# A weight's sign and rounded tail in one word, its sum on VectorE or GpSimd, and a new order of issue, in an attention and softplus-FFN kernel

## The chip, the cores and the metric

The kernel runs on one core of a Trainium2 chip. The metric is the device time of one execution in microseconds (us), the median of several runs. The core has five engines with a queue each: TensorE (PE, matrix products), VectorE (DVE), ScalarE (ACT), GpSimd (POOL) and SyncE (SP, which here issues every DMA). They run side by side and wait for one another through semaphores. Each queue is strictly in order: an instruction that waits holds up everything behind it.

## The reference

```python
# q, k, v: (4, 8, 768, 64) float32; block = 32, window = 16
k_sum = k.reshape(B, H, nb, block, D).max(axis=3)          # 24 block keys: the maximum
v_sum = v.reshape(B, H, nb, block, D).mean(axis=3)         # 24 block values: the mean
scores_l = where(|i - j| < window, scale * q @ k.T, -1e9)
scores_s = scale * q @ k_sum.T + log(block)
a = softmax(concatenate([scores_l, scores_s]))             # over 768 + 24 keys
x = (a @ concatenate([v, v_sum])).reshape(3072, 512)       # the heads side by side
h = x @ w_in                                               # 512 x 2048
g = maximum(h, 0) + log1p(exp(-abs(h)))                    # softplus
out = g @ w_out                                            # 2048 x 512
```

`w_in` and `w_out` arrive as 64-bit floats, two 32-bit words an element; all else is float32.

## The kernel before

**Chunks and phases.** The 3072 tokens are 12 chunks of 256. A group of one or two chunks is fed forward together: groups `[0,1] [2] [3,4] [5,6] [7,8] [9,10] [11]`, numbered x = 0 to 6. The hidden dimension is cut into 16 slices of 128, f = 0 to 15. For each group and slice TensorE makes `ph = w_in[f]·x` (L845, `product`), ScalarE the softplus twice from PSUM (`gh` rounded, L868, and the exact one, L872), VectorE the difference `gl` (L876, `rest`), and TensorE adds `g·w_out[f]` into `po` (L883, `project`). Operands are split into a high and a low part (`xh`, `xl`; `gh`, `gl`; the weight `w` in two halves), and each product takes three matmuls. Below, "f0.10" is slice 10 of group 0. Groups 0 and 1 go through slices 0 to 10 first and come back for 11 to 15, since the weights are still being converted.

**Attention.** A unit is one chunk with four of the eight heads: scores (`sc`, L612), mask and row minimum on VectorE (L625), exp on ScalarE (L633), the inverse of the sum (L641), normalizing on VectorE or GpSimd (L646), a transpose, values (`xo`, L706), then `xh` and `xl` (L722, L729). The four units of group 0 (a0.0.0, a0.0.2, a0.1.0, a0.1.2) transpose on TensorE (`pt`, L659) and copy to `pT` (L663); later units go through DRAM (`squares`). The first product of the kernel needs a0.0.0 and half of w0. Until then TensorE's gaps are filled with `warm` products (L965).

**Weights.** For each f the function `weights` loads w_in[f] and w_out[f] as raw words (L755, L758; for f = 0 and 1 separately, 512 columns each; from f = 2 together, 1024 columns) and makes a float32 by integer steps: magnitude (mask of the upper word, L771 on VectorE or L774 on ScalarE), `clamp` (L778), `shift` left by 3 (L782), `sign` (L786, the sign and top exponent bit of the upper word, or-ed in), `tail` (L792 on ScalarE or L795 on VectorE: the lower word over 2^29, rounded to 0..8, in place), `add_tail` (L800, GpSimd: an exact integer add), `high` (L804, a rounding copy into `w`) and `low` (L811, the remainder, on VectorE or GpSimd). The raw words of w6 to w15 lie where the first group's attention keeps its inputs, so these loads come after it. Temporaries (`t` of the weights, `kf`, `st`, `ob`) share a ring of two buffers, tag "t"; a load into the ring waits in SP's queue until the buffer two before it is free.

**Order.** Every step is a `Task` with one or several ways (engine and function). `SEQUENCE`, a table of 1623 numbers, is the order in which the tasks are issued; a letter after a number takes the second or third way ("a", "b"). DMAs go round eight semaphores, so each waits until the one eight before it has landed.

Of the kernel before, what the change touches and what calls it, by code (L numbers as in the profile page):

```python
# [12 lines left out]
U32 = mybir.dt.uint32  # L13
I32 = mybir.dt.int32
# [133 lines left out]
43 44 0 3 4 5 6 2 7 154 155 156 157 145 158 159 160 8 45 146a 46 9 10 11 12 13 14 15 82 64 68 16 17 150 147 148  # L148
161 149 162 18 19 163 151 20 144 47 49 21 22 23 78 51 164a 168 24 25 92 93 48 152 94 26 27 28 29 1 30 165 166
167 50 169 170 172 177 95 52 31 153 96 173a 104 105 106 174 171 53 175 176 55 72 54 56 75 116 97 98 99 117 118  # L150
59 57 100 61 58 60 62 89 86 128 63 85b 32 71b 81b 604 178 107 108a 181 179a 180 119 33 109 34 35 111 36 37 38
605 129 120 67 182 183 184 185 186 39 40 65 69 70 66 101 130 131 187 188 417 41 608 609 83 80 84 79 191 192 140
141 142 424 425 77b 102 103 110 112 76 87 74b 189 426 73 438 42 201 113 114a 115 190 616 143 202 321 335 336 121
122 132 123 124 193 194 195 427 196 322 323 125 126a 127 324 325 428 133 445 134a 617 90 197 198 622 624 135 349
88b 211 337 338 339 91b 136 418 419 212 207 221 326 222 423 203 204 205 206 328 350 137 138 351 352 327 340 139
429 421 342 446 208 199 329 330 343 430 341 353 354 200a 331 332 333 344 345 612 251 431 434 420 346 209 210 355
623 433 432 213 214 215 216 447 448 217a 356 357 449a 231 232 358 334 361 362 363 613 364 347 422 621 348 359
360 367 365 223 224 630a 218 366 225 227 219 220 625 368 371 226 228 369 435 370 241 450 633 372 233a 234 235
237 229 242 252 436 451 236 439 441 230 444 261 262 452 437 648 243a 238 244 245 246 373 379 374 375 377 247 647
380 381 376 378 248 382 271 272 440 291 651 239 240 249 250 253 254 255 256 257 383 384 263a 385 634 391 386 387  # L160
388 264 265 258 656 649 392 389 390 395 266 259 260 650 393 394 277 267 442 453 443 454 455 456 457 268 659 458
269a 270 397 396 403 311 606 607a 635 398 399 636 401 400 610 674 611a 678 404 405 614 281 618 626 637 615 406
402 638 459 660 465 292 629 619 460 466 467 461 462 410 407 411a 468 409 408 412a 293 661 662 294 620 675 282
413 312 471 463 464 469 470 472 473 295 477 297 478 479 475 474 483 484 485 476 481 296 663a 298 299 480 486 301
673 273 274 639 489 490 491 275 276 492 664 482 495 496 497 498 278 487 488 493 494 501 507 279 300 502 503 414
415a 280a 508 504 681 283 284 287 509 628 640 510 513 499 514 317 515 285 286 500 505 302 519 516 520 631 643
528 521 288 506 289 511 512 517 696 416 697 700a 641 695 682 518 703 824 823 825 665 303 304 305 529 627 290 826
# [17 lines left out]
1070 1278a 1271 822 976 974 977 1076 975 1071 1089 1088 1090 978 979 980 982 988 1079 1111 1133 1134 1135 983
989 984 1272 990 985 1078 1260 991 981 986 1091 1092 1258 1259 1269 1273 1112 1281 1136a 1137 1093 1282 1283
1284 994 987 1000 992 995 993 1001 996 1285a 997 998 1295 1296 1099 1100 1298 999 1113 1101 1115 1138 1286 1002
1003 1261 1004 1005 1006 1007 1008 1009 1012 1013 1102 1116 1014 1304a 1299 1105 1104 1114 1117 1125 1139 1140
1287 1130 1141 1118 1119 1015 1010 1011 1128 1018 1127 1016 1131 1126 1019 1017 1024 1297 1307 1020 1025 1021
# [17 lines left out]
1465 1526 1468 1464 1469 1535 1536 1527 1466a 1528 1533 1532 1537 1538 1541 1542 1543 1544 1547 1548 1549 1534  # L207
# [8 lines left out]
def kernel(  # L216
# [521 lines left out]
    def weights(f):  # L738
        order.group = f"w{f}"

        for i0, i1 in [(0, 1), (1, 2)] if f < 2 else [(0, 2)]:
# [19 lines left out]
            def word(up, dtype, raw=raw):  # L761
                return raw()[:, :, up].bitcast(dtype)
# [22 lines left out]
            def sign(t=t, word=word):  # L785
                nc.vector.scalar_tensor_tensor(  # L786
                    t(), word(1, U32), 0xC0000000, t(), ALU.bitwise_and, ALU.bitwise_or,
                )
# [255 lines left out]
```

## Time and profile before

| | |
|---|---|
| median of 3 runs | 620.74 us (620.58 to 621.48) |
| the profiled execution | 621.56 us, of which the span from first to last instruction is 619.8 us |
| TensorE busy | 608.5 us (98%), granted clock 0.994 in the mean |
| VectorE, ScalarE, GpSimd busy | 273.8 us (44%), 306.8 us (50%), 95.3 us (15%) |
| `add_tail` on GpSimd (L800) | 18 instructions, 41.8 us |
| `sign` on VectorE (L786) | 18 instructions, 19.8 us |
| bytes moved by DMA | 85.33 MB |

Busy time is time with an instruction running. A matmul counts as busy while it waits in the array, so the share of TensorE says little; whether it has gaps is read from the start times of its products. The page's lines by stage show that VectorE and ScalarE are full in the first 100 us and half idle later.

### The profile page before, as it was taken

Reading aid. Unit: us, or ns where it says so; the run is one execution under the profiler, and the core shown is the slowest. Engines: PE = TensorE matmul, PEld = TensorE weight load, DVE = VectorE, ACT = ScalarE, POOL = GpSimd, SP = SyncE. Lnnn points to the kernel's source line nnn. Section 1 sums busy time; section 2 is a strip of 40 time slices with the busy share of each in tenths; the row PEclk is TensorE's granted clock in tenths of the full one; section 3 lists DMA queues with packets and bytes.
Section 4 is the critical chain, followed back from the end, with each engine's and each line's share of the span. In section 5 each row is a group of like instructions: output and inputs, shape, how many; then the busy total and the mean of one; then the engine's idle time right before and its main releaser. Section 6 shows DMA issues by size and latency. Waiting matters only on the chain.

```text
span 619.8 us, 11379 instructions
## 1 busy us (share of the span) xinstructions
PE 608.5 (98%) x4384; PEld 506.8 (82%) x4384; DVE 273.8 (44%) x752; ACT 306.8 (50%) x758; POOL 95.3 (15%) x86
## 2 busy tenths in 40 slices
PE   7989999999999999999999999999999999999997
PEld 6678888988888888888888888888888888888996
DVE  5999997777454335544235221321333202211111
ACT  4998786748463255656637234631354314312322
POOL 4454533543100010112102004000000000000000
PEclk8899999999999999999999999999999999999999
DMA  9888985843557356464436145340533200210100
GB/s 304 252 272 275 316 266 132 268 139 113 160 186 255 96 160 191 118 210 145 144 117 207 38 142 123 88 128 1 143 98 106 73 1 2 76 59 0 69 1 34
DMA packets 83765, 85.33 MB, mean 138 GB/s; under 512 B 24608, under 2 KB 69504, under 8 KB 83712
## 3 DMA queue, kind: packets, MB, share of 16 engines
q1 hardware_dynamic: 83712, 84.62, 44.6%
q8 instruction: 34, 0.56, 0.4%
q14 instruction: 19, 0.16, 0.1%
HBM read 64.23 MB, written 18.35 MB: 133 GB/s over the span
## 4 chain that ended last, share of the span: by engine, by line
PE 78%; issue 1%; POOL 1%; ACT 0%; DVE 0%; POOLq 0%
PE po L883 37%; PE ph L845 36%; PE xo L706 3%; PE sc L612 2%; POOL t L800 1%; POOL w L811 0%; ACT ob L926 0%; DVE gl L876 0%; POOLq L800 0%; POOLq L811 0%
## 5 line engine op out<-in xcount | busy, mean ns | idle before, releaser
L845 PE MATMUL ph<-xh,w 128*128 128x512 f32 (+1 forms) x920 | 259.5, 355 | 1.0 <-DVE gl L876 0.9
L883 PE MATMUL po<-w,gh 128*128 128x512 f32 x768 | 201.4, 392 | 0.0
L845 PEld LDWEIGHTS ph<-xh,w 128*128 128x128 f32 x920 | 164.9, 189 | 27.6 <-DVE gl L876 1.7
L868 ACT ACTIVATE gh<-ph 128x512 fp32r<-128x512 f32 (+1 forms) x115 | 60.7, 528 | 230.3 <-PE ph L845 210.8
L876 DVE TENSOR_TENSOR gl<-ph,gh 128x512 fp32r<-128x512 f32 (+1 forms) x115 | 68.2, 599 | 233.7 <-ACT ph L872 233.1
L883 PEld LDWEIGHTS po<-w,gh 128*128 128x128 f32 x768 | 142.5, 188 | 29.9 <-issue 0.3
L845 PE MATMUL ph<-xl,w 128*128 128x512 f32 (+1 forms) x460 | 163.0, 354 | 0.4 <-DVE xl L729 0.4
L883 PE MATMUL po<-w,gl 128*128 128x512 f32 x384 | 113.5, 392 | 0.0
L845 PEld LDWEIGHTS ph<-xl,w 128*128 128x128 f32 x460 | 86.8, 189 | 13.4 <-DVE xl L729 0.6
L883 PEld LDWEIGHTS po<-w,gl 128*128 128x128 f32 x384 | 70.8, 188 | 14.4 <-DVE t L782 0.2
L633 ACT ACTIVATE sp<-sp,nm 128x120 f32<-128x120 f32 x192 | 73.1, 382 | 1.2 <-DVE nm L625 0.9
L872 ACT ACTIVATE ph<-ph 128x512 f32<-128x512 f32 (+1 forms) x115 | 59.0, 520 | 0.0
L800 POOL TENSOR_TENSOR t<-t,raw 128x1024 int32<-128x1024 int32 (+1 forms) x18 | 41.8, 2323 | 65.7 <-DVE t L786 16.1
L625 DVE CUSTOM_DVE_ANT_0 sp<-sc,added 128x120 f32<-128x120 f32 x192 | 40.7, 277 | 10.9 <-PE sc L612 10.6
L646 POOL TENSOR_TENSOR sp<-sp,ss 128x960 f32<-128x960 f32 x12 | 22.6, 1881 | 99.6 <-DVE ss L641 99.6
L633 ACT ACTIVATION_READ_ACCUMULATOR sp<-sp,nm 128x1 f32 x192 | 35.9, 187 | 0.0
L729 DVE TENSOR_TENSOR xl<-xo,xh 128x512 fp32r<-128x512 f32 x24 | 16.4, 682 | 37.5 <-ACT xh L722 37.3
L363 POOL TENSOR_TENSOR st<-st 96x512 f32<-96x512 f32 (+1 forms) x14 | 14.1, 1010 | 120.5 <-DMA st<-v_hp_dram 54.2
L868 ACT ACT_TABLE_LOAD x21 | 26.9, 1283 | 9.8 <-PE ph L845 9.5
L722 ACT CAST xh<-xo 128x512 fp32r<-128x512 f32 x22 | 12.9, 587 | 32.2 <-PE xo L706 32.2
L633 ACT ACT_TABLE_LOAD x18 | 23.1, 1283 | 7.4 <-DVE nm L625 7.2
L675 DVE STREAM_TRANSPOSE tb<-sp 128x1024 f32<-128x1024 f32 x20 | 24.8, 1238 | 1.5 <-POOL sp L646 1.1
(70 smaller groups left out, 391.8 us busy)
## 6 DMA issues: line engine op xcount, KB each, us to landing
squares<-tb SPq DMA_DIRECT2D x20, 512.0 KB
pT<-squares SPq DMA_DIRECT2D x80, 128.0 KB
raw<-w_out_dram SPq DMA_DIRECT2D x16, 512.0 KB
raw<-w_in_dram SPq DMA_DIRECT2D x16, 512.0 KB
kf<-kT_dram SPq DMA_DIRECT2D x16, 384.0 KB
out_dram<-ob SPq DMA_DIRECT2D x11, 512.0 KB
q<-qT_dram SPq DMA_DIRECT2D x20, 256.0 KB
st<-v_hp_dram SPq DMA_DIRECT2D x12, 384.0 KB
```

The lines of the kernel that those rows point to most:

```text
L625: nc.vector.tensor_tensor_reduce(out=sp()[:, n], in0=unit(n), in1=added()[:, kinds.index((lows[w], lows[w + 1]))], scale=-SCALE, scalar=FL ...
L633: nc.scalar.activation(sp()[:, n], sp()[:, n], AF.Exp, bias=nm()[:, n:n + 1], scale=-1.0, accum_out=ss()[:, n:n + 1],)
L646: engine.tensor_tensor(sp(), sp(), s, op=ALU.mult)
L675: nc.vector.transpose(out=tb().rearrange("p k (u q) -> p u k q", q=SQ), in_=tiles.sp().rearrange("p u (k q) -> p u k q", q=SQ),)
L706: nc.tensor.matmul(xo()[h * D:(h + 1) * D, g * CH + w * QW:g * CH + (w + 1) * QW], lhsT=tiles.v(g)[:, w, h * D:(h + 1) * D], rhs=queries(g ...
L729: nc.vector.tensor_sub(out=of_x(xl), in0=of_bank(), in1=of_x(xh).bitcast(F32))
L800: nc.gpsimd.tensor_tensor(a, a, word(0, I32), op=ALU.add)
L845: nc.tensor.matmul(ph()[:, :n], lhsT=w1()[:, i1, low, cc * P:(cc + 1) * P], rhs=a()[:, cc, cols], start=cc == 0 and i == 0, stop=cc == NCC ...
L868: nc.scalar.activation(gh()[:, cols], ph()[:, :n], AF.Softplus)
L872: nc.scalar.activation(ph()[:, :n], ph()[:, :n], AF.Softplus)
L876: nc.vector.tensor_sub(out=gl()[:, cols], in0=ph()[:, :n], in1=gh()[:, cols].bitcast(F32))
L883: nc.tensor.matmul(po[t](), lhsT=a()[:, t * P:(t + 1) * P], rhs=w2()[:, i2, low], start=f == f0 and i == 0, stop=f == f1 - 1 and i == 2,)
```

## The change

The upper raw word is reduced in place to its top two bits (`sign`, now a one-source instruction that writes `raw`). The rounded tail, 0..8, is written as 16 bits into the low half of the same word (`rounded_tail`). One integer add then puts both onto `t`. Before, sign and tail came in by two instructions from two words. The add has a second way, on VectorE, where it is built as one custom instruction over the 16-bit halves; 8 of the 18 adds take it. `tail` now writes the word that `magnitude` and `sign` use, so it has to follow both; before it hung on its load alone.

```diff
+U16 = mybir.dt.uint16
 ...
-            def sign(t=t, word=word):
-                nc.vector.scalar_tensor_tensor(
-                    t(), word(1, U32), 0xC0000000, t(), ALU.bitwise_and, ALU.bitwise_or,
-                )
-            order.add(DVE, dve(n), sign, upper, [t], port=True)
+            def sign(word=word):
+                nc.vector.tensor_scalar(word(1, U32), word(1, U32), 0xC0000000, None, ALU.bitwise_and)
+            order.add(DVE, dve(n, double=True), sign, [], upper, port=True)
 
-            def tail(word=word):
-                nc.scalar.activation(word(0, I32), word(0, U32), AF.Copy, scale=2.0 ** -29)
-            def tail_by_vector(word=word):
-                nc.vector.tensor_scalar(word(0, I32), word(0, U32), 2.0 ** -29, None, ALU.mult)
-            order.add(ACT, act(n), tail, [], lower, ways=[Way(DVE, dve(n), tail_by_vector, port=True)])
+            def rounded_tail(raw=raw):
+                return raw()[:, :, 1:].bitcast(U16)[:, :, 0]
+            def tail(word=word, to=rounded_tail):
+                nc.scalar.activation(to(), word(0, U32), AF.Copy, scale=2.0 ** -29)
+            def tail_by_vector(word=word, to=rounded_tail):
+                nc.vector.tensor_scalar(to(), word(0, U32), 2.0 ** -29, None, ALU.mult)
+            order.add(ACT, act(n), tail, lower, upper, ways=[Way(DVE, dve(n), tail_by_vector, port=True)])
 
-            def add_tail(t=t, word=word):
+            def add_tail(engine, t=t, word=word):
                 a = t().bitcast(I32)
-                nc.gpsimd.tensor_tensor(a, a, word(0, I32), op=ALU.add)
-            order.add(POOL, pool(n), add_tail, lower, [t])
+                engine.tensor_tensor(a, a, word(1, I32), op=ALU.add)
+            order.add(
+                POOL, pool(n), lambda f=add_tail: f(nc.gpsimd), upper, [t],
+                ways=[Way(DVE, 0.16 + 0.0013 * n, lambda f=add_tail: f(nc.vector), port=True)],
+            )
```

`SEQUENCE` is replaced as a whole; its first line shows how little can be read from it:

```diff
-43 44 0 3 4 5 6 2 7 154 155 156 157 145 158 159 160 8 45 146a 46 9 10 11 12 13 14 15 82 64 68 16 17 150 147 148
+0 3 1 172 173a 4 43 44 176 177 163 5 6 7 8 174 175 178a 164a 179 2 165 167 168 9 166 10 11 12 13 14 15 16 45 46
```

Three places show what the new table moves. First SP's queue before the loads of the first values. `kf<-kT_dram` at L349 is a load into the "t" ring, for the second batch's block keys; `first<-v_hp_dram` are the values that the first `xo` needs. Before:

```order
L550 DMA first<-qT_dram 128x256 x2
L349 DMA kf<-kT_dram 128x768
L758 DMA raw<-w_in_dram 128x4x256
L755 DMA raw<-w_out_dram 128x1024
L559 DMA first<-v_hp_dram 96x128 x2
L559 DMA first<-v_hp_dram 96x3x128 x2
```

The same place in the new order:

```order
L759 DMA raw<-w_in_dram 128x4x256
L756 DMA raw<-w_out_dram 128x1024
L409 DMA vn_220<-v_hp_dram 128x4x128
L409 DMA vn_419<-v_hp_dram 128x4x128 x2
L551 DMA first<-qT_dram 128x256 x2
L560 DMA first<-v_hp_dram 96x3x128 x2
L560 DMA first<-v_hp_dram 96x128 x2
L492 DMA q<-qT_dram 128x512
L350 DMA kf<-kT_dram 128x768
```

The ring's load now stands behind the first values instead of ahead of them, and w2 is loaded ahead of the last three `vn` loads. At the very start SP now loads half of w1 ahead of the first keys.

Second, VectorE at the conversion of w8, w9 and w10, the last weights before the product f0.10. Before (w10's steps, then w9's and w10's `low`):

```order
L876 TENSOR_TENSOR gl<-ph,gh 128x512
L778 TENSOR_SCALAR t<-t 128x1024
L782 TENSOR_SCALAR t<-t 128x1024
L514 COPY k<-ks 128x8x24
L786 SCALAR_TENSOR_TENSOR t<-raw,t 128x1024
L811 TENSOR_TENSOR w<-t,w 128x2x512
L876 TENSOR_TENSOR gl<-ph,gh 128x512
L729 TENSOR_TENSOR xl<-xo,xh 128x2x256
L804 CAST w<-t 128x2x512
L811 TENSOR_TENSOR w<-t,w 128x2x512
```

And now (w9's `high` and `low`, then w10's steps):

```order
L809 CAST w<-t 128x2x512
L816 TENSOR_TENSOR w<-t,w 128x2x512
L772 TENSOR_SCALAR t<-raw 128x1024
L787 TENSOR_SCALAR raw<-raw 128x1024
L779 TENSOR_SCALAR t<-t 128x1024
L783 TENSOR_SCALAR t<-t 128x1024
L802 ISA t<-raw,t 128x2048
L809 CAST w<-t 128x2x512
```

`sign` has become a one-source instruction (L787), the add has come to VectorE (L802, 2048 halves of 1024 words), and w10's `low` has left it.

Third, GpSimd between the first attention and the block sums of the second batch. Before:

```order
L646 TENSOR_TENSOR sp<-sp,ss 128x8x120
L800 TENSOR_TENSOR t<-t,raw 128x1024 x2
L811 TENSOR_TENSOR w<-t,w 128x2x512
L800 TENSOR_TENSOR t<-t,raw 128x1024 x6
L646 TENSOR_TENSOR sp<-sp,ss 128x8x120
```

And now:

```order
L647 TENSOR_TENSOR sp<-sp,ss 128x8x120
L802 TENSOR_TENSOR t<-t,raw 128x1024 x3
L647 TENSOR_TENSOR sp<-sp,ss 128x8x120
L816 TENSOR_TENSOR w<-t,w 128x2x512
L802 TENSOR_TENSOR t<-t,raw 128x1024 x2
L816 TENSOR_TENSOR w<-t,w 128x2x512
```

Of eight adds five are left here, and w6's and w10's `low` have come in their place.

More of the change, by code (lines that the diff above doesn't have):

```diff
@@ L153 @@
[L153 to L167, printed above, removed]
@@ L185 @@
[L185 to L189, printed above, removed]
@@ new lines @@
+107 117 53 54 181 182 183 96 97 186 118 56 99 57 108a 160 119 161 162 184 185 59 61 187 58 60 62 98 100a 63 67b
+85b 89 86 128 129 109 71 70 66 69 65 101 110a 111 39 40 130 188 189 81 417 102a 604 84 80 103 605 41 112 120 42
+424 425 83 79 113 191 114a 140 143 192 87 121 438 141 73 115 321 335 74 76 336 426 190a 211 608 131 132a 427 428
+193a 196 212 77b 322 323 324 197 337 123 445 122a 124a 125 325 194 195 198 126 127 338 91b 88b 349 326 339 609
+133 134 135 350 136 213 214 327 215 216 90 418 419 423 622 199 137 138 139 200 351 352 217 429 340 328 329 341
@@ new lines @@
+330 331 630a 332 420 142 201 624 202 218 203 206 204 231 232 353 430 219 354 342 343 623 421 344 333 355 345 207
+205 208 221 334 222 220 346 431 433 434 356 432 357 446 358 422 233a 447 347 348 359 361 360 209a 210 367 236
+223 226 261 224 225 448 449 362 363 365 368 369 364 370 227 228a 237 229 234 373 625 230a 235 435 621 633 450
+634 374 436 375 366 281 371 372 376 437 635 238 379 241 242 648 451 239a 240 377 385 243 246 247 380 244 245 381
+248a 249 439 442 441 606 251 607a 382 250 378 282 252 452 440 616 444 253 651 386 387 383 256 254 384 257 391
@@ new lines @@
+392 455 393 262 255 388 617 258 394 612 389 390 259a 395 647 260 397 263 266 267 264 265 268a 269a 613 453 398
+399 400 396 270a 636 637a 454 401 649 443 456 650 656a 659 457 458 610 614 611a 403 404 615 405 301 626 627 618
+311 402 459 460 406 407 302 408 461 465 466 638 462 660 411 412a 413 409 619a 467 410 471 463 464 472 473 620
+283 468 286 287 284 474 285 288 312 271 632 272 469 477 478 479 483 484 485 414a 480 415a 470 486 289 416 489
+475 476 290 481 482 495 490 491 492 273 276 277a 274 639 291 275 674 675 678a 303a 306 304 305 496 487 497 498
@@ new lines @@
+629 640 307a 278a 501 488 493 494 499 500 507 308 673 502 505 503 508 279 509 504 506 510 309 280 513 519 310
+514 520 681 292 511 512 696 700 515 521 516 293 294 517 661 697 522 528 518 313a 295 296 297a 529 530 536 537
+298a 538 523 524 299a 300 662 663 631 531 532 542 316 525 317 533 539 642 695 548 314 641 526 315 534 318a 535
+543 319a 544 545 664 320a 628 643 549 550 682 554 562 665 527 551 644 683 652 655 654 684 685 703 657 658 666
+668 669 653 667 686 824 704 832a 687 540 541 546 547 823 827 552 553 555 556 645 557 826 825 670 646 676 679 688
@@ new lines @@
+803 809 1061 804 1062a 1063 1077 805 806 940 924 1253 925 1080 1081 1064 1256 941 1065 1067 802 810 811 1053
+1054 942 1082 1095 1103a 807 808 812 943 1264 1057 944 952 1083 945 946 1094 813 814 947 815 816 1084 1257 820
+1068 1056 821 953 1066 1096 1098 1097 1106 1069 1085 1265 1086 950 1087 1088 817a 818 1075 1078 948 949 951 1089
+954 1070 1071 955 958 959 960 1107 961 1108 1090 1121 1109 956 964 970 957 965 1076 962 822 963 1110 1079 1111
+819 1122 971 1124 966 967 968 976 972 1112 973 977 978 979 982 1123 1120 1129a 1132 983 984 1091 1099 1100 1105
@@ new lines @@
+1104 969 1113 1116 1102 1254 1092 1093 985 1114 1260 1270 974 975 980 981 988 1278a 989 990 1101 1115 986 987
+994 992 1133 1134 991 1117 1272 1271 1273 1269 1281 1296 1261 995 1304 996 1125 1135 1255a 997 1298 1000 1258
+1118 1119 1001 1127 1128 1002 1003 1136 1006 1007 1008 993 1012 1009 998 999 1013 1004 1259a 1137 1282 1283 1284
+1014 1285 1131 1138 1286 1015 1295 1287 1139 1005 1266 1010 1018 1011 1016 1019 1020 1017 1024 1025 1021 1022
+1030 1262 1031 1023 1028 1026 1027 1263a 1036 1032 1033 1130 1142 1126 1029 1140 1141 1143 1299 1297 1307 1267
@@ new lines @@
+1144 1037 1038 1288 1321 1308 1039 1034 1035 1042 1040 1047a 1145 1044 1043 1041 1048a 1146 1154 1268 1147 1148
+1149 1155 1156 1322 1291 1290 1323 1289 1274 1277 1280 1276 1326 1160 1045a 1157 1166 1152 1150 1161 1049 1162
+1163 1151 1172 1153 1158 1159 1164 1309 1310 1311 1165 1167 1173 1312 1174 1168 1169 1275 1279 1292 1293 1294
+1329 1313 1314 1170 1171 1300 1302 1305 1315 1306 1175 1046 1344 1345 1178 1184 1179 1180 1181 1176 1185 1186
+1187 1190 1177 1191 1192 1182 1196 1183 1188 1189 1301 1194 1330 1317 1331 1193 1348a 1197 1332 1316 1303 1343
@@ new lines @@
+1318 1333a 1351 1198 1199 1319 1471 1324 1334 1352 1320 1195 1200 1472 1202 1203 1204 1205 1208 1209 1201 1210
+1327 1211 1480 1214 1353 1354 1215 1206 1207 1335 1216 1217 1328 1220 1221 1212 1336 1338 1473 1339 1475 1222
+1474 1483 1325 1337 1340 1341 1346 1350 1349 1223 1355a 1356 1484 1357 1498 1342 1500 1499 1213 1226 1232 1358
+1218 1361 1485 1227 1219 1359 1347 1233 1234 1228 1229 1235 1486 1501 1224 1225 1230 1231 1238 1506 1360 1362
+1497 1509 1363 1236 1364 1237 1239 1240 1241 1242 1243 1244 1249 1365 1245 1250a 1251 1476 1373 1246 1366 1367
```

41 lines of the change are left out of this document (15 added, 26 removed), and 25 rows, old and new, of the table SEQUENCE.

## The prediction

> **What bounds the kernel now.** I read the busy times by stage first, then the chain of waits, TensorE's own waits, and last the start of each queue in order of time. The stages (time, then busy time of PE, PEld, DVE, ACT and POOL with their counts, clock, DMA share, GB/s):
>
> ```profile
> 0.00:36.83 36.83, 31.09 (x492) 23.99 (x492) 28.61 (x116) 26.64 (x87) 17.20 (x35) 0.91 0.87 279
> 36.83:99.60 62.77, 61.81 (x534) 52.18 (x531) 57.84 (x105) 52.63 (x99) 27.69 (x11) 1.00 0.83 259
> 99.60:140.00 40.40, 39.48 (x264) 35.12 (x263) 30.30 (x79) 25.24 (x63) 18.07 (x13) 1.00 0.68 197
> 140.00:619.80 479.80, 476.08 (x3101) 395.53 (x3099) 157.00 (x456) 202.31 (x510) 32.35 (x28) 1.00 0.35 106
> ```
>
> After 140 us VectorE works 157 of 480 us; between 36.83 and 99.60 it works 57.84 of 62.77. The weights fall into the first 150 us, so what the change does to VectorE and GpSimd can matter only there. The page's chain that ended last:
>
> ```profile
> PE 78%; issue 1%; POOL 1%; ACT 0%; DVE 0%; POOLq 0%
> ```
>
> TensorE carries it. Its waits after the first product, all of them, and the rows of the products on which the sum below stands:
>
> ```profile
> PE ph L845 <- DVE gl L876: 0.9, 1, 0.9
> PE pt L659 <- DVE xl L729: 0.5, 1, 0.5
> PE ph L845 <- DVE xl L729: 0.4, 1, 0.4
> 35.73 1.18 PE L706 MATMUL xo<-pT,first 120*64 120x64 f32 x32 [0.38 <-ACT pT L663]
> 36.83 0.39 PE L845 MATMUL ph<-xh,w 128*128 128x256 f32 x1
> 101.06 0.39 PE L845 MATMUL ph<-xh,w 128*128 128x512 f32 x1
> 132.48 0.39 PE L845 MATMUL ph<-xh,w 128*128 128x256 f32 x1 [0.92 <-DVE gl L876]
> ```
>
> The first product (L845) starts at 36.83 us, f0.10's at 101.06, and from 36.83 to the end TensorE waits 1.8 us in all, 0.9 of it at 132.48. Nearly everything that can be won is therefore the start, 36.83 us, and these 1.8 us; everything that can be lost is a weight or a start that comes late. The products are the same in number and size in both kernels.
>
> **The start.** The queue that issues the loads, and the DMA engines, between 16 and 28 us:
>
> ```profile
> 22.26 0.33 SPq L349 DMA_DIRECT2D kf<-kT_dram  x1
> 21.49 0.69 DVE L811 TENSOR_TENSOR w<-t,w 128x512 fp32r<-128x512 f32 x1
> 16.00:20.00 4.00, 4.00 (x70) 2.51 (x69) 3.40 (x10) 3.29 (x12) 2.73 (x2) 0.66 0.98 301
> 20.00:24.00 4.00, 3.95 (x76) 2.37 (x75) 3.97 (x27) 3.66 (x18) 1.24 (x2) 1.00 0.36 111
> 24.00:28.00 4.00, 4.00 (x73) 2.04 (x72) 3.86 (x18) 3.98 (x18) 0.77 (x2) 1.00 0.90 298
> ```
>
> SP's load into the "t" ring at 22.26 us comes right after VectorE's `low` that ends at 22.18: it was waiting for that buffer, and the first values were queued behind it. Meanwhile the DMA engines fell to 111 GB/s from 301. In the new order that load stands behind the values. The hole costs 4 x (301 - 111)/301 = 2.5 us of transfer: at most that much is won.
>
> It isn't all won, since the row at 35.73 shows the last values before the first product waiting for ScalarE's `pT` copy, not for a load. ScalarE's work ahead of that copy, by these rows:
>
> ```profile
> L722 ACT CAST xh<-xo 128x512 fp32r<-128x512 f32 x22 | 12.9, 587 | 32.2 <-PE xo L706 32.2
> L804 ACT CAST w<-t 128x1024 fp32r<-128x1024 f32 x12 | 12.6, 1050 | 4.9 <-POOL t L800 4.9
> L564 ACT COPY first<-vn 24x512 f32<-24x512 f32 x7 | 4.1, 615 | 0.1
> L663 ACT COPY pT<-pt 120x512 f32<-120x512 f32 x7 | 3.9, 584 | 0.4 <-PE pt L659 0.3
> L804 ACT CAST w<-t 128x512 fp32r<-128x512 f32 x3 | 1.8, 614 | 0.7 <-POOL t L800 0.7
> ```
>
> Two `pT` copies (2 x 0.58), two copies to `first` (2 x 0.62) and one `xh` (0.59) leave it, w2's `high` (1.05) and one 512-column `high` (0.61) come: -1.3 us. On VectorE ahead of the same place two adds, two `pT` copies and one cast come, two 512-column `low`, the dearer part of five signs, one cast and one block maximum go; within half a microsecond these cancel. Against it, the first keys are now queued behind 512 KiB of w1:
>
> ```profile
> 3.96 0.95 DVE L335 TENSOR_REDUCE ks<-kf 128x24 f32<-128x768 f32 x1 [3.96 <-DMA kf<-kT_dram]
> 5.54 0.43 DVE L771 TENSOR_SCALAR t<-raw 128x512 uint32<-128x512 uint32 x1 [0.63 <-DMA raw<-w_out_dram]
> ```
>
> VectorE's first work moves from the first landing (3.96) to about the second (5.54), 1.6 us later, which the idle time that follows can absorb. So the first product moves by -2.5 to +1.6; between VectorE's 0 and ScalarE's -1.3 I take **-0.6**. One half-unit of `pt` transposes also moves from behind the first product into the `warm` gap ahead of it:
>
> ```profile
> 39.72 1.03 PE L659 MATMUL pt<-ident,sp 128*120 128x128 f32 x8
> ```
>
> Half of 1.03 is **-0.5** (0 if the start isn't waiting there). Of the 1.8 us of waits I take half, **-0.9** (bounds -1.8 and +2): the one at 132.48 is `gl` held up behind a ring buffer, and the new order can meet the like elsewhere. By TensorE's side the sum is -2.0 us.
>
> **VectorE up to w10.** This is the tightest place: does VectorE get the weights done? Start-to-start times show what an instruction costs it:
>
> ```profile
> 11.33 0.69 DVE L786 SCALAR_TENSOR_TENSOR t<-raw,t 128x512 uint32<-128x512 uint32 x1
> 11.94 0.68 DVE L811 TENSOR_TENSOR w<-t,w 128x512 fp32r<-128x512 f32 x1
> 32.21 0.69 DVE L782 TENSOR_SCALAR t<-t 128x1024 uint32<-128x1024 uint32 x1
> 32.94 1.23 DVE L786 SCALAR_TENSOR_TENSOR t<-raw,t 128x1024 uint32<-128x1024 uint32 x1
> 34.08 0.16 DVE L640 TENSOR_SCALAR ss<-ss 128x8 f32<-128x8 f32 x1
> 45.15 0.68 DVE L663 COPY pT<-pt 120x512 f32<-120x512 f32 x1
> 45.74 0.94 DVE L335 TENSOR_REDUCE ks<-kf 128x24 f32<-128x768 f32 x1
> 97.66 0.68 DVE L804 CAST w<-t 128x1024 fp32r<-128x1024 f32 x1
> 98.38 1.22 DVE L811 TENSOR_TENSOR w<-t,w 128x1024 fp32r<-128x1024 f32 x1
> 99.52 1.14 DVE L363 TENSOR_TENSOR st<-st 96x512 f32<-96x512 f32 x2
> L811 POOL TENSOR_TENSOR w<-t,w 128x1024 fp32r<-128x1024 f32 x2 | 4.8, 2405 | 1.2 <-ACT w L804 1.2
> L811 DVE TENSOR_TENSOR w<-t,w 128x512 fp32r<-128x512 f32 x4 | 2.7, 675 | 0.0
> ```
>
> `sign` goes from 34.08 - 32.94 = 1.14 to the 0.73 of `shift` (32.94 - 32.21), a one-source instruction on the same tile; with 512 columns from 0.61 (11.94 - 11.33) to about 0.46. No row shows the new add. It streams 2048 halves, the bytes of 1024 words. The nearest rows are `low`, two sources: 1.22 us at 1024 columns and 0.675 at 512, so 1.06 ns a column, and 2.3 us if each half counts as a column. Bounds 1.2 and 2.3; I take 1.5, nearer to the row with the same bytes (0.85 for 512 columns). The tail's 16-bit output I price at nothing on either engine: its input is unchanged; bounds 0 and +0.6 each.
>
> Up to w10's last VectorE step the new order against the old: nine and four signs -9 x 0.41 - 4 x 0.15 = -4.3; adds 3 x 1.5 + 2 x 0.85 = +6.2; two `low` of each size gone, -2 x 1.14 - 2 x 0.6 = -3.5; three more casts of 0.72 and one small one fewer, +1.7; three more `pT` copies of 0.6, +1.8; one block-value sum (99.52 and what follows), +1.5; one block maximum -0.9; small things -1.0. Together +1.5. And w10's `low` now follows on GpSimd, +2.4 (2405 ns). Before, it ended at 98.38 + 1.22 = 99.6, 1.5 us ahead of the product. Unchanged idle time would make that 103.5. In the new order 8 projections of f0.9 come ahead of f0.10's product (1.8) and the 0.5 above has been done earlier, so at the old pace TensorE asks for w10 at 102.4.
>
> VectorE's idle time to 99.6 is 36.83 - 28.61 = 8.2 plus 62.77 - 57.84 = 4.9. Following the new order by hand with these durations, the start leaves 6.4 (early signs and four block maxima fill waits for keys); of the later 4.9 I take off 1.1, an estimate, for loads that are there sooner: idle falls by 2.9, w10 is ready at 100.6, which allows -1.8. Together with TensorE's -2.0 I take **-1.9**.
>
> How VectorE and GpSimd meet shows here:
>
> ```profile
> 74.54 3.22 POOL L800 TENSOR_TENSOR t<-t,raw 128x1024 int32<-128x1024 int32 x1 [2.78 <-DVE t L786]
> 76.67 1.64 DVE L778 TENSOR_SCALAR t<-t 128x1024 f32<-128x1024 f32 x1 [0.61 <-ACT t L774]
> ```
>
> `clamp`, otherwise 0.7 us, took 1.64 and ended 0.55 after GpSimd's add did. [...]
>
> **After w10.** From 99.6 to 140 VectorE idles 40.40 - 30.30 = 10.1 us, and the new order puts some 4 us more ahead of f0.11's `rest` (w11's and w13's adds of 1.5, two tails of some 0.6). The idle time hides it; if not, up to +2. After 140: the same work, no waits before, 0 (bounds -0.3 and +0.7).
>
> **Sum.** 621.56 (the profiled execution: 619.8 of span and 1.8 around it) - 1.9 = 619.7. It lay 0.82 above the median 620.74, so 618.8 us in terms of the median. About 0.2%, 1.24 us, is what a measurement of this kernel can tell from no change: faster is below 619.5, slower above 622.0.
>
> **Rivals.**
> - *VectorE becomes the bound at w10 (slower).* If the late first keys cost it their 1.6 us and no idle time is absorbed, w10 is ready at 105.1 against 102.4 and TensorE stalls 2.7: 621.56 + 2.7 - 0.82 = 623.4. It decides when idle shrinks by less than 1.1 us. For it: 92% busy in the stage. Against: half of the idle time lies in the start, which is rearranged. 0.13.
> - *The add costs 2.3 (slower).* Three of 1024 and two of 512 columns cost 3 x 0.8 + 2 x 0.4 = 3.2 more; w10 at 103.8, +1.4: 622.1. For it: the instruction counts 2048 elements. Against: the same bytes. 0.12. [...]
> - *Nothing moves.* The start gains nothing (ScalarE's relief is eaten by the longer chain magnitude, sign, tail, add) and the stalls change places: -0.5, 620.2. For it: both engines are full from 20 us on. 0.20.
>
> **How the numbers follow.** Forecast 0.55, its own range 616.9 to 619.5 (start -2.5, half the waits and the transposes as the low end). Faster 0.55 plus a little of the third, slower most of the first two. The range 616.7 to 622.6 takes in the add at 2.3 and the first 2 us of a VectorE that is late; it leaves out the rest of that rival (some 0.1), and all of the 2.5 us hole won with all waits gone (0.05).
>
> **What would show it.** Right: first product at about 36.2 us; no hole in the DMA rate at 20 to 24; L787 at 0.7 us; the add near 1.5; f0.10's product near 100.5 with no wait on `w`. Wrong: the add's row at 2.3; a TensorE wait on GpSimd's `w` or on VectorE near f0.6 to f0.15; a first product later than 37.5; or new gaps after 140.

## The result: 1.6% slower

The changed kernel takes 631.27 us, median of 4 runs (630.99 to 631.75), against 621.11 of the kernel before beside it; the ratio is 1.0162, 95% interval 1.0144 to 1.0179. The profiled execution has a span of 629.2 us against 619.8: 9.4 us more.

The stages after, with the same borders as those of before but for the first product, which starts at 36.34 instead of 36.83 (time, busy time of PE, PEld, DVE, ACT and POOL, clock, DMA share, GB/s), and the start of the loads:

```profile
0.00:36.34 36.34, 28.65 (x496) 22.26 (x497) 28.80 (x118) 29.04 (x89) 18.19 (x37) 1.00 0.86 278
36.34:99.60 63.26, 58.97 (x458) 48.29 (x457) 51.97 (x103) 52.06 (x95) 20.45 (x9) 1.00 0.78 240
99.60:140.00 40.40, 39.42 (x282) 34.18 (x282) 33.08 (x67) 20.76 (x34) 11.01 (x7) 1.00 0.66 206
140.00:629.20 489.20, 481.45 (x3155) 400.54 (x3153) 170.63 (x493) 208.73 (x528) 27.47 (x21) 1.00 0.36 106
20.00:24.00 4.00, 4.00 (x59) 1.86 (x49) 3.76 (x23) 4.00 (x18) 1.26 (x1) 1.00 1.15 326
24.00:28.00 4.00, 3.87 (x70) 1.69 (x68) 3.90 (x8) 4.00 (x10) 0.03 (x1) 1.00 0.23 64
```

Between 36 and 99.6 VectorE now works 51.97 us where it worked 57.84, and yet TensorE is busy only 58.97 of 63.26. TensorE's waits behind the first product, those over 0.2 us, and below them the page's chain:

```profile
PE ph L850 <- DVE gl L881: 4.1, 1, 4.1
PE po L888 <- ACT gh L873: 2.2, 3, 1.0
PE pt L660 <- DVE xl L730: 0.7, 1, 0.7
PE po L888 <- DVE gl L881: 0.7, 1, 0.7
PE ph L850 <- DVE w L809: 0.6, 1, 0.6
PE ph L850 <- DVE w L816: 0.5, 1, 0.5
PE 84%; DVE 4%; ACT 4%; DMA 3%; issue 3%; SPq 2%; POOL 0%; POOLq 0%; ACTq 0%
```

Before, the same view had 1.8 us in three waits; now the first line alone has 4.1 in one, and the second names ScalarE, which stood in no line of before. The page's chain is still TensorE's, but ACT and VectorE take 4% each of it.

A wait holds only what TensorE stood still, not the slow instructions behind it. So this tally, too: for each TensorE instruction the time to the next start, less the mean of its kind (its shape) in the kernel before, added up to a given time (us; the end is the last start). The mean leaves out the shortest and the longest twentieth of each kind, so that the kernel before has a tally too.

```
up to          40     60     85    110    140    340    360    end
before        7.2    9.1    9.6   10.1   11.6   17.6   17.9   21.1
after         5.7    9.5   10.6   15.4   15.7   21.3   27.6   30.6
difference   -1.5   +0.4   +1.0   +5.3   +4.1   +3.7   +9.7   +9.5
```

So 1.5 us are won ahead of 40; 6.8 are lost between 40 and 110; 1.2 come back up to 140 (the wait at 132.48 is gone); and 6.0 are lost between 340 and 360. There are two losses, and nothing else of size.

**The loss from 40 to 110.** The weights' groups (line, engine, operation, tiles, shape, count | busy us, mean ns | idle time ahead of them):

```profile
L794 ACT ACTIVATE raw<-raw 128x1024 uint16<-128x1024 uint32 x11 | 27.8, 2554 | 12.4 <-DVE raw L787 12.3
L794 ACT ACTIVATE raw<-raw 128x512 uint16<-128x512 uint32 x3 | 4.0, 1347 | 2.0 <-DVE raw L787 1.9
L797 DVE TENSOR_SCALAR raw<-raw 128x1024 uint16<-128x1024 uint32 x3 | 4.0, 1341 | 0.1
L802 DVE CUSTOM_DVE_ANT_0 t<-raw,t 128x2048 uint16<-128x2048 uint16 x6 | 7.4, 1232 | 5.0 <-ACT raw L794 5.0
L787 DVE TENSOR_SCALAR raw<-raw 128x1024 uint32<-128x1024 uint32 x14 | 11.0, 787 | 0.2
```

In the kernel before the tail's groups were:

```profile
L792 ACT ACTIVATE raw<-raw 128x1024 int32<-128x1024 uint32 x13 | 15.0, 1160 | 0.1
L792 ACT ACTIVATE raw<-raw 128x512 int32<-128x512 uint32 x4 | 2.7, 670 | 3.5 <-DMA raw<-w_out_dram 3.5
L795 DVE TENSOR_SCALAR raw<-raw 128x1024 int32<-128x1024 uint32 x1 | 0.6, 643 | 0.0
```

ScalarE's tail went from 1.16 to 2.55 us, with 512 columns from 0.67 to 1.35; VectorE's from 0.64 to 1.34. The input is the same; the output differs, a 16-bit half of every second word in place of the whole word. And the idle time ahead of it now names VectorE's sign (L787, 12.3 us): the tail shares the sign's word and has to follow it. ScalarE's queue at two of the waits, and TensorE's instruction that waited:

```profile
82.81 2.53 ACT L794 ACTIVATE raw<-raw 128x1024 uint16<-128x1024 uint32 x1 [2.35 <-DVE raw L787]
85.36 1.28 ACT L873 ACT_TABLE_LOAD   x1
86.65 0.60 ACT L873 ACTIVATE gh<-ph 128x512 fp32r<-128x512 f32 x1
87.30 1.89 PE L888 MATMUL po<-w,gh 128*128 128x512 f32 x7 [0.94 <-ACT gh L873]
100.88 2.53 ACT L794 ACTIVATE raw<-raw 128x1024 uint16<-128x1024 uint32 x1 [5.15 <-DVE raw L787]
103.14 0.70 ACT L873 ACTIVATE gh<-ph 128x512 fp32r<-128x512 f32 x1
103.89 1.43 PE L888 MATMUL po<-w,gh 128*128 128x512 f32 x5 [0.98 <-ACT gh L873]
```

Both times the tail (L794) runs 2.5 us ahead of the softplus (L873) whose `gh` TensorE wants, the first time with a table load between them. The tail holds up the weights as well: VectorE's adds (L802) stood idle for 5.0 us waiting for it, and the two waits of TensorE for `w` (at 98.2 and 99.4) stand behind such a chain, with the add on GpSimd.

**The loss at 349.** The softplus that the rest needs, VectorE's queue and TensorE's:

```profile
342.86 0.59 ACT L877 ACTIVATE ph<-ph 128x512 f32<-128x512 f32 x1
344.86 0.26 DVE L515 COPY k<-ks 128x192 f32<-128x192 f32 x1 [6.67 <-PE sc L613]
345.35 2.56 DVE L364 TENSOR_TENSOR st<-st 96x512 f32<-96x512 f32 x2
348.16 0.68 DVE L881 TENSOR_TENSOR gl<-ph,gh 128x512 fp32r<-128x512 f32 x1
343.74 1.05 PE L613 MATMUL sc<-k,q 64*64 64x120 f32 x32
348.89 0.50 PE L850 MATMUL ph<-xh,w 128*128 128x512 f32 x1 [4.10 <-DVE gl L881]
```

The `rest` of the product f3.8 (L881) had its input at 343.45 (342.86 + 0.59), but on VectorE it stands behind the copy of the key sums (L515), which waits 6.7 us for TensorE's scores (343.74), and behind two block-value sums (L364). TensorE's next product wants the bank that this `rest` frees. So TensorE does the scores and then stands still for 4.1 us until VectorE has worked off what waited for those scores. It pays once more behind it:

```profile
349.00:352.60 3.60, 3.60 (x10) 2.82 (x11) 0.43 (x1) 0.00 (x0) 0.00 (x0) 0.54 0.39 104
352.60:356.00 3.40, 3.40 (x16) 2.85 (x15) 0.69 (x1) 1.09 (x2) 0.00 (x0) 0.99 0.00 0
```

The granted clock is 0.54 for 3.6 us, and by the tally another 1.6 us are lost between 349 and 353.

### The profile page after: what moved, and what is told of

The parts are those of the page before. It is cut to its first block, busy times and chain, and to the rows that moved or that the text cites. A ratio compares the mean times of both kernels' runs of the same rounds, so it can differ in the third digit from the quotient of the medians.

```text
span 629.2 us, 11374 instructions
## 1 busy us (share of the span) xinstructions
PE 608.5 (97%) x4384; PEld 505.3 (80%) x4384; DVE 284.5 (45%) x778; ACT 310.6 (49%) x743; POOL 77.1 (12%) x73
## 4 chain that ended last, share of the span: by engine, by line
PE 84%; DVE 4%; ACT 4%; DMA 3%; issue 3%; SPq 2%; POOL 0%; POOLq 0%; ACTq 0%
PE po L888 39%; PE ph L850 39%; PE xo L707 3%; PE sc L613 3%; DMA vn<-v_hp_dram 1%; ACT raw L794 1%; DMA first<-v_hp_dram 1%; DVE t L772 1%; DMA pT<-squares 1%; DVE raw L787 1%; ACT sp L634 0%; DVE gl L881 0%; ACT L873 0%; ACT gh L873 0%; DVE st L364 0%
## 5 line engine op out<-in xcount | busy, mean ns | idle before, releaser
L873 ACT ACTIVATE gh<-ph 128x512 fp32r<-128x512 f32 (+1 forms) x115 | 61.3, 534 | 216.4 <-PE ph L850 199.6
L881 DVE TENSOR_TENSOR gl<-ph,gh 128x512 fp32r<-128x512 f32 (+1 forms) x115 | 68.1, 598 | 210.0 <-ACT ph L877 210.0
L647 POOL TENSOR_TENSOR sp<-sp,ss 128x960 f32<-128x960 f32 x13 | 23.9, 1836 | 287.5 <-DVE ss L642 282.5
L794 ACT ACTIVATE raw<-raw 128x1024 uint16<-128x1024 uint32 (+1 forms) x14 | 31.9, 2295 | 14.4 <-DVE raw L787 14.2
L676 DVE STREAM_TRANSPOSE tb<-sp 128x1024 f32<-128x1024 f32 x20 | 24.8, 1240 | 10.1 <-POOL sp L647 9.9
L802 POOL TENSOR_TENSOR t<-t,raw 128x1024 int32<-128x1024 int32 (+1 forms) x10 | 22.8, 2284 | 52.9 <-ACT raw L794 39.8
L730 DVE TENSOR_TENSOR xl<-xo,xh 128x512 fp32r<-128x512 f32 x24 | 16.5, 688 | 27.8 <-ACT xh L723 27.8
L707 PEld LDWEIGHTS xo<-pT,v 120*64 120x64 f32 x640 | 20.3, 138 | 5.7 <-issue 5.3
```

Of the source, the lines that this page charges most:

```text
L647: engine.tensor_tensor(sp(), sp(), s, op=ALU.mult)
L676: nc.vector.transpose(out=tb().rearrange("p k (u q) -> p u k q", q=SQ), in_=tiles.sp().rearrange("p u (k q) -> p u k q", q=SQ),)
L707: nc.tensor.matmul(xo()[h * D:(h + 1) * D, g * CH + w * QW:g * CH + (w + 1) * QW], lhsT=tiles.v(g)[:, w, h * D:(h + 1) * D], rhs=queries(g ...
L794: nc.scalar.activation(to(), word(0, U32), AF.Copy, scale=2.0 ** -29)
L802: engine.tensor_tensor(a, a, word(1, I32), op=ALU.add)
L873: nc.scalar.activation(gh()[:, cols], ph()[:, :n], AF.Softplus)
```

## The experiments

Eleven kernels ran; ratios are to the kernel before on the same chip.

**The 32-bit tail in the changed kernel.**

```
-  return raw()[:, :, 1:].bitcast(U16)[:, :, 0]                      # where the tail goes
+  return raw()[:, :, 0].bitcast(I32)
-  engine.tensor_tensor(a, a, word(1, I32), op=ALU.add)
+  engine.tensor_tensor(a, a, word(0, I32), op=ALU.add)
```

> The changed kernel with one edit: the rounded tail is written as a 32-bit word into the lower word, as the kernel before writes it, and the add takes the lower word (the sign stays in the upper word and is left out of the result). Order, engines and instruction count are those of the changed kernel. Theory T (the 16-bit write makes ScalarE's tail 2.55 us where the 32-bit one takes 1.16, and the tail stands ahead of the softplus that TensorE waits for): the tail's row falls to about 1.16, the TensorE waits on gh at 59.6, 87.3 and 103.9 go, the lost time between 45 and 110 falls by 4 to 6 us, and the time is 625 to 627. The 4.1 us wait at 349 stays. Theory O (the new order itself brings the stalls, whatever the tail takes): 630 to 631.5, the waits stay.

The sign's instruction runs, but the sign doesn't reach the result. 624.8 us, 1.0053 (1.0038 to 1.0068), 6.5 less than the changed kernel and just under what theory T expected. The tail's row and TensorE's waits between 42 and 330:

```profile
L794 ACT ACTIVATE raw<-raw 128x1024 int32<-128x1024 uint32 x11 | 12.6, 1159 | 1.8 <-DMA raw<-w_out_dram 1.8
PE ph L850 <- DVE xl L730: 0.2, 1, 0.2
```

Of the waits in that stretch 0.2 us are left, and the tally up to 110 falls from 15.4 to 8.2, below the 10.1 of before. The first product comes at 34.1 us. The 4.1 us wait (here at 341) stayed, and the clock behind it was 0.50 for 6.7 us (340.8 to 347.5), so that by the tally 7.6 us are lost there.

Theory T holds against theory O, but this edit takes out two things at once. The tail is short again, and in the lower word it no longer has to follow the sign: its idle time names its load (1.8 us) where the changed kernel's names the sign (12.3). At 90 us it starts 3.2 us ahead of its sign. Which of the two counts is told by the words side by side, below.

**The rest ahead of the copy.** In the sequence, with 995 and 996 the softplus and 997 the rest of f3.8, 1304 the copy:

```
-  ... 995 1304 996 1125 1135 1255a 997 ...
+  ... 995 996 997 1304 1125 1135 1255a ...
```

> The changed kernel with one edit of the order: the softplus and the rest of the product f3.8 are issued ahead of the copy of the key sums for a5.0.2, so that on VectorE this rest no longer stands behind a copy that waits for TensorE's scores and behind two block-value sums. Theory (the 349 us wait is a queue made by the order: the copy waits for the scores, the next product for a bank that the rest behind the copy frees): the 4.1 us wait goes, with it the eight products at half rate behind it (1.4 us), and the time falls by 5 to 6 to 625.5 to 626.5. Rival (the wait only moves: the scores or the exponent after them are late next): 629 to 631.

627.16 us, 1.0088 (1.0070 to 1.0105): 4.1 less, not 5 to 6. The wait went, but one product later there is another:

```profile
PE ph L848 <- DVE xl L728: 1.2, 1, 1.2
```

The rounding rest `xl` of the values a4.1.0 was next in the same queue, behind the same two sums. The theory holds for the wait, and the rival for 1.2 us of it.

**The words of before in the changed order.** Sign by a two-source instruction into the shifted word, 32-bit tail, adds on the changed kernel's engines:

```
-  nc.vector.tensor_scalar(word(1, U32), word(1, U32), 0xC0000000, None, ALU.bitwise_and)
+  nc.vector.scalar_tensor_tensor(t(), word(1, U32), 0xC0000000, t(), ALU.bitwise_and, ALU.bitwise_or)
```

> The changed kernel's order and its adds on VectorE, with the words of before: the sign goes by a two-source instruction into the shifted word (it is issued behind the shift where it stood ahead of it), the tail is a 32-bit word, and both ways of the add take that word. Theory T: the tail is the only thing that costs: 625 to 627, as with the 32-bit tail alone. Rival V (the one-source sign was needed: VectorE has 14 x 0.5 + 4 x 0.2 = 7.8 us more to do, most of it ahead of w10): TensorE waits for VectorE's weights near 95 to 110, 628 to 631.

632.41 us, 1.0167 (1.0147 to 1.0187), no better than the changed kernel, though the tail is short. VectorE's sign is 1.37 us on average here, and TensorE waits for VectorE, above all at 51.8, 55.2 and 81.3:

```profile
L785 DVE SCALAR_TENSOR_TENSOR t<-raw,t 128x1024 uint32<-128x1024 uint32 x14 | 19.2, 1372 | 0.5
PE ph L847 <- DVE gl L878: 3.1, 3, 1.7
PE ph L847 <- DVE xl L728: 1.9, 1, 1.9
PE po L885 <- DVE gl L878: 1.5, 2, 1.1
```

Theory T missed and rival V has the direction: the new order needs the cheap sign. But the time is above V's 631, and the waits are on `xl` and `gl` up to 81 us, not on weights near 95 to 110; V had the place wrong. The sign's price and its later place, behind the shift, are not told apart here.

**The same with the rest ahead.** 996 and 997 ahead of 1304, as in the second run.

> The last kernel with the rest of f3.8 moved ahead as well. If the tail's width and the queue at 349 are two causes that add up, this saves 5 + 5.5 on 631.3 and lies at 619 to 621, at or under the kernel before (whose start it beats by 1.5 us and whose wait at 132 it lacks). If a third cause is left in the new order: 622 to 626.

627.46 us, 1.0099 (1.0080 to 1.0117): 5 us less than without it, as the theory of the queue has it. It lies above both expected ranges, which counted the tail's 5 us as won; VectorE's sign takes them, as above.

**Both losses taken out.** The 32-bit tail as in the first run (the sign doesn't reach the result, and the tail doesn't wait for it), and ahead of the copy the four instructions 996, 997, 1118 and 1119 (`xl` of a4.1.0).

```
+  return raw()[:, :, 0].bitcast(I32)                                # and the add takes word(0)
+  ... 995 996 997 1118 1119 1304 1125 1135 1255a ...
```

> The changed kernel with both causes taken out: the 32-bit tail in the lower word (the sign is left out of the result, as in the run with the tail alone), and ahead of the key-sum copy of a5.0.2 the softplus and rest of f3.8 and also the rounding and rest of the values a4.1.0, which the run with the rest alone showed to be late next (1.2 us on xl). Two causes and no third: the run with the 32-bit tail lost 7.4 us at 341, so 624.8 - 7.4 = 617.4, with 619.5 as the upper end, under the kernel before (621.7). A third cause in the new order: 621 or more.

617.96 us, 0.9943 (0.9925 to 0.9960). TensorE's waits from 36 us to the end:

```profile
PE po L886 <- DVE gl L879: 1.4, 1, 1.4
PE ph L848 <- DVE xl L728: 0.5, 1, 0.5
```

With a short tail and no queue at 349, as my sum had assumed, the change brings 3.1 us; the forecast was 618.8. The tally is 4.1 at 40, 8.6 at 110 and 17.8 at the end, and it rises by nothing between 340 and 360. No third loss shows in the changed kernel.

**The new words in the order of before.** The sign's mask keeps the low half (`0xC000FFFF`), all adds on GpSimd:

```
-  nc.vector.scalar_tensor_tensor(t(), word(1, U32), 0xC0000000, t(), ALU.bitwise_and, ALU.bitwise_or)
+  nc.vector.tensor_scalar(word(1, U32), word(1, U32), 0xC000FFFF, None, ALU.bitwise_and)
-  nc.scalar.activation(word(0, I32), word(0, U32), AF.Copy, scale=2.0 ** -29)
+  nc.scalar.activation(raw()[:, :, 1:].bitcast(U16)[:, :, 0], word(0, U32), AF.Copy, scale=2.0 ** -29)
-  nc.gpsimd.tensor_tensor(a, a, word(0, I32), op=ALU.add)
+  nc.gpsimd.tensor_tensor(a, a, word(1, I32), op=ALU.add)
```

> The kernel before with the new words alone: its order (four of the tails are put just behind their magnitude), all adds on GpSimd; the sign masks the upper word in place (the mask keeps the low half, so that it may stand behind the tail) and the tail is a 16-bit half of that word. Theory T: each large ScalarE tail costs 1.4 us more, some 17 us of ScalarE work in the first 145 us, in an order laid out for the short one: TensorE waits for softplus there, 624 to 628. Rival: VectorE's cheaper sign (14 x 0.5 us) and ScalarE's idle time there hide it: 621 to 622.5.

643.62 us, 1.0360 (1.0338 to 1.0381): the direction of T, far beyond its size. Besides the 1.4 us of each tail there is a wait that I had not priced. The half goes into the upper word, and the trace has the tail wait for the sign (L785) and the magnitude (L770) that use this word. These waits of ScalarE from 20 to 110:

```profile
ACT raw L792 <- DVE raw L785: 4.9, 2, 4.0
ACT raw L792 <- DVE t L770: 2.8, 2, 2.3
```

Before, the tail only needed its load. So this run doesn't tell the longer tail from its longer chain. The first product comes at 39.3 us, f0.10's at 116.7.

**The words of before for four weights.** w4, w8, w9 and w10, with the four instructions ahead of the copy:

```
+  WORDS_OF_BEFORE = (4, 8, 9, 10)
+  if f in WORDS_OF_BEFORE:      # two-source sign into t, 32-bit tail, the add takes word(0)
```

> The changed kernel with the words of before (two-source sign behind the shift, 32-bit tail) for w4, w8, w9 and w10 alone, whose long tails stood ahead of the softplus at 59, 87, 95 and 103 us, and with the four instructions moved ahead of the key-sum copy at 349; adds stay on their engines. If these four tails made the waits: the lost time up to 110 falls from 15.4 to 11 or 12, and the time is 620.5 to 622.5. If VectorE has no room for four two-source signs (0.5 us each) or the other tails are as bad: 624 to 626.

624.31 us, 1.0045 (1.0028 to 1.0062). The second reading holds: four shorter tails gave only 1 us up to 110 (14.5). No wait on `gh` is left, but these on VectorE have come, as in the third run:

```profile
PE po L907 <- DVE gl L900: 2.7, 3, 1.4
```

The rest of the gain is the queue at 349.

**A list of prices.** The tail's copy of 1024 words (every second 32-bit word of a tile), behind the last product, into a tile of its own:

```
+  nc.scalar.activation(out_of(zx, form), pairs(wx)[:, :, 0], AF.Copy, scale=2.0 ** -29)
+  nc.vector.tensor_scalar(out_of(zy, form), pairs(wy)[:, :, 0], 2.0 ** -29, None, ALU.mult)
```

> The changed kernel with a list of prices behind its last product (no part of the result): the tail's scaled copy of 1024 32-bit words of every second word, twice on ScalarE and twice on VectorE, into five places of a tile of its own: every second 32-bit word; the low half of every second word (the changed kernel's form); 32-bit words side by side; 16-bit halves side by side; the low halves of words side by side. If the partial write into a word is what costs: 1.16 us on ScalarE for the 32-bit forms and for the halves side by side, 2.5 for both forms of half words. If any 16-bit result costs: 2.5 for all three 16-bit forms. If the distance costs: 2.5 only where every second word is written.

One of each form, in this order: every second word; the low half of every second word; words side by side; halves side by side; halves of words side by side (4 bytes apart). Each row is a stretch with its busy time; five of ScalarE, then VectorE's first, second and last form:

```profile
632.11:633.28 1.17, 1.14 (x1) 0.50 0.00 0
636.85:639.38 2.53, 2.50 (x2) 0.50 0.00 0
640.55:641.73 1.18, 1.15 (x2) 0.50 0.00 0
642.89:644.03 1.14, 1.11 (x2) 0.50 0.00 0
645.40:646.80 1.40, 1.34 (x1) 0.50 0.00 0
633.86:634.58 0.72, 0.70 (x1) 0.50 0.00 0
636.54:637.87 1.33, 1.31 (x1) 0.50 0.00 0
641.58:642.40 0.82, 0.75 (x1) 0.50 0.00 0
```

VectorE's third and fourth form take 0.69 each. Neither the 16 bits (1.11 side by side) nor the distance (1.14 for words 8 bytes apart) costs by itself; 16-bit pieces 8 bytes apart do (2.50), and 4 bytes apart little (1.34). None of the three readings holds as it stands: the first has 2.5 us for halves 4 bytes apart, where 1.34 was measured, the second 2.5 for every 16-bit result, and the third 2.5 for words 8 bytes apart too. At the same distance of 8 bytes the halves take 2.2 times as long as the words (2.50 against 1.14).

**Words side by side, from w4 on.** The shared word goes into tiles that are free at that time (the places of w14 and w15), 4 bytes apart; the four instructions are ahead of the copy.

```
+  for u in (14, 15):
+      both = buffer([P, 2, 2 * DM], U32, "both", f"w{u}", 1, wts)
+      side.extend([(both, 0), (both, 1)])
-  nc.vector.tensor_scalar(word(1, U32), word(1, U32), 0xC0000000, None, ALU.bitwise_and)
+  nc.vector.tensor_scalar(both(U32), word(1, U32), 0xC0000000, None, ALU.bitwise_and)
-  return raw()[:, :, 1:].bitcast(U16)[:, :, 0]
+  return both(U16).rearrange("p (n two) -> p n two", two=2)[:, :, 0]
-  engine.tensor_tensor(a, a, word(1, I32), op=ALU.add)
+  engine.tensor_tensor(a, a, both(I32), op=ALU.add)
```

> A complete version that follows the price list: for w4 to w10 the shared word (sign and tail) is no longer every second word of the raw weights but lies side by side with its neighbours in two tiles that are free between the first attention and the last weights' loads, so that ScalarE's tail writes a half of every word 4 bytes apart (1.34 us in the list instead of 2.49). The four instructions are ahead of the key-sum copy at 349 as well; all else is the changed kernel, with w2 and w3 (tails at 26 and 42 us) as they are. If the distance of the halves was what cost: seven tails of 1.2 us less, the waits on gh at 59, 87 and 103 go, the lost time up to 110 falls to 9 or 10, and the time is 618 to 620, under both the kernel before (621.1) and the changed one. If the two early tails, or the reads of the new tiles, weigh as much: 621 to 624.

619.41 us, 0.9981 (0.9971 to 0.9992). The seven tails take 1.38 us; the waits on `gh` are gone, and the tally up to 110 is 10.1, as before.

```profile
L805 ACT ACTIVATE both<-raw 128x1024 uint16<-128x1024 uint32 x7 | 9.5, 1384 | 9.5 <-DVE both L796 9.4
```

These tails still wait for the sign (9.4 us of idle time), as in the changed kernel. What changed for ScalarE is their length, and from 40 to 110 the tally rises by 3.8 us (6.3 to 10.1), where the changed kernel's rises by 9.7 and that of before by 2.9. So the length makes 5.9 of the 6.8 us of the first loss, and the wait for the sign little of it; VectorE's own tails of the changed form are still in this run.

**All adds on GpSimd.** The last kernel with the eight adds marked "a" without the mark, nothing else:

```
-  178a 151a 228a 248a 268a 278a 298a 318a
+  178  151  228  248  268  278  298  318
```

> The same with every add on GpSimd (eight adds leave VectorE, nothing else differs): what the way on VectorE is worth by itself. An add takes 2.53 us there against 1.23 on VectorE and holds VectorE up meanwhile; w6, w8 and w10 come 1.3 us later each, and w11's and w13's too. If that matters: TensorE waits on w near 90 to 105, 1 to 3 us more. If the weights have that much room: within 0.5 us of the version above.

629.63 us, 1.0146 (1.0126 to 1.0166): 10.2 us more, far above my 1 to 3. My estimate took in w6 to w13 only. Two small adds of w0 and w1 go to GpSimd too, and 3.6 us are lost in the start: the first product comes at 40.1 us instead of 36.5. TensorE stands still there for 4.4 us ahead of a scores instruction, and the trace names no engine for it. The queues show where the time goes. GpSimd's first add, at 8.37 us, waits 6.4 us for ScalarE's tail, and behind it stands the mask that the scores need: it is done at 14.2 us instead of 6.5. The second add follows it, at 14.27 instead of 11.14; ScalarE's `high` waits 3.5 us for that add; and the exponents behind `high` start at 17.40 instead of 14.28. That is 3.1 of the 3.6 us, read from the trace and not taken out by a run. By f0.10 the difference is 5.1 (107.8 against 102.7), the rest follows later. So this order needs these adds on VectorE, but the 10.2 us are not the adds' length alone. That GpSimd's add holds VectorE up meanwhile is measured in single rows only: in the changed kernel, beside the add of 53.02 to 55.46 us VectorE's mask (L772) took 2.21 us, against 0.69 in eight of its ten rows, and ended 0.55 after the add; but `xl` (L730), inside the add of 45.10 to 47.51, took its usual 0.69.

**Words side by side for w0 to w3 as well**, in the places of w2 to w5 before their loads:

```
+  u = {(0, 0): 4, (0, 1): 5, (1, 0): 3, (1, 1): 2, (2, 0): 4, (3, 0): 4}[f, i0]
+  here = buffer([P, 1, n], U32, "early", f"w{u}", 1, wts), 0
```

> The complete version with the side-by-side words for w0 to w3 too (in the places of w2 to w5 before their loads; w11 to w15 stay as in the changed kernel). The version with 32-bit tails everywhere had its first product at 34.2 us, the one with side-by-side words from w4 on at 36.5: if the early tails (three of 1.35 and two of 2.54 us on a ScalarE that is full from 16 to 40 us) make this difference, the first product comes at 34.5 to 35, and the time is 617.5 to 618.5, under the version before it (619.4). If the start is set by something else (the keys, the transposes): first product at 36 or later, 619 to 620.

617.02 us, 0.9930 (0.9913 to 0.9947), the fastest of all and a little under what was expected: 4.2 us under the kernel before, 14 under the changed one. The early tails:

```profile
L810 ACT ACTIVATE early<-raw 128x1024 uint16<-128x1024 uint32 x2 | 2.7, 1374 | 0.0
L810 ACT ACTIVATE early<-raw 128x512 uint16<-128x512 uint32 x3 | 2.3, 779 | 2.4 <-DVE early L801 2.3
```

Here the sign reaches the result and the early tails keep their wait for it. The first product starts at 34.2 us, f0.10's at 99.4; the tally is 4.1 at 40, 6.8 at 110, 16.0 at the end.

## Why the prediction was wrong

The sum gave 618.8 us, 1.9 less than before; 10.2 more were measured. Two terms that the sum held at about zero were not.

- *The step that failed first:* "The tail's 16-bit output I price at nothing on either engine: its input is unchanged; bounds 0 and +0.6 each". It measured +1.39 for each of ScalarE's eleven large tails, +0.68 for each of the three small ones, 17 us of ScalarE in all, and +0.7 on VectorE for each of its three large ones. The trace of before had no row of a 16-bit write at this distance, so the upper bound was no bound. And the sum had VectorE's side up to w10 and TensorE's, but none of ScalarE's after the start: there was no term in which a longer tail could have shown. Taken out together with the tail's wait for the sign, it gives back 6.5 us; shortened with that wait left in place, it gives back 5.9 of the 6.8 us lost between 40 and 110.
- *The step that failed second:* "After 140: the same work, no waits before, 0 (bounds -0.3 and +0.7)". It measured 6.0: the same work in another order is not the same queue. The order showed it: between one product and the next stood the scores, and on VectorE the copy that needs them ahead of the rest that the product needs. I named "new gaps after 140" as a sign of being wrong and did not go through the queues there.
- *First product, -0.6 (bounds -2.5 and +1.6):* measured -0.5, which is luck. The hole at 20 to 24 us is closed (326 GB/s against 111), but another follows (64 at 24 to 28). With short tails the first product comes at 34.1 or 34.2, 2.6 to 2.8 us earlier than before and so beyond the bound of 2.5; the long tails ate 2 of it. The -0.5 of the transposes was not measured by itself.
- *The add, 1.5 (bounds 1.2 and 2.3):* 1.23, the lower bound. The rival of 2.3 falls: 1.23 is beside the row with the same bytes (1.22).
- *The sign, 0.73:* 0.68 to 0.70 for thirteen of the fourteen at 1024 columns; the one at 151.68 us, beside GpSimd's normalizing (151.33 to 153.12), took 2.00, so that the mean is 0.79.
- *VectorE up to w10, ready at 100.6, f0.10's product near 100.5:* w10's `low` on GpSimd ended at 108.0 and the product came at 108.0. With the 32-bit tail they came at 99.9 and 100.7, with no wait on `w`. So VectorE had room for the new work, as the sum said, but the weights hung on ScalarE's tail, which the sum left out; and that run's first product was 2 us earlier than the sum's.
- *Half the waits, -0.9:* the one at 132.48 is gone, but with both losses out 1.9 us of waits are left behind the first product, as many as before; by that the term is 0.
- *The rivals:* in none was ScalarE the engine that comes late. "Nothing moves" came nearest in kind, with its relief "eaten by the longer chain magnitude, sign, tail, add".

With both losses out, 617.96 was measured against 618.8 forecast. That this is so near is partly luck: by the tally 3.1 us are won ahead of 40, where the sum had 1.1 (start and transposes), 1.6 are lost again by 110, and 1.9 come back later.

## What to carry to other kernels

Price an instruction by the pattern that it writes, not only by what it reads: a row with another output type or step is not its row (here 2.55 us against 1.16), and if the trace has none, run the form once behind the kernel, in a list of prices. When an order changes, follow each engine's queue over its whole length and ask at each instruction that waits for the bottleneck what the bottleneck wants from behind it; work that is the same can stand in another place. And make a sum for every engine that feeds the bottleneck, not just for the one that is full.

## What was not expected of the hardware

A 16-bit result written 8 bytes apart takes ScalarE 2.50 us for 1024 columns against 1.11 side by side, 1.34 at 4 bytes, and 1.14 for 32-bit results 8 bytes apart; VectorE 1.31 against 0.69, 0.75 and 0.70. And after TensorE had stood still for 4.1 us its granted clock was 0.54 for 3.6 us (0.50 for 6.7 us behind the same wait in the first run); around its waits of up to 1 us between 59 and 104 it was 1.00.
